# Gate logits of five token tiles as VectorE products instead of TensorE products, in an attention, MLP and mixture-of-experts kernel

## The chip, the cores and the metric

The kernel runs on one core of a Trainium2 chip. The metric is the device time of one launch in microseconds. Five engines work from queues of their own: TensorE (PE in the profile; its weight loads are PEld), VectorE (DVE), ScalarE (ACT), GpSimd (POOL) and SyncE (SP, which here only issues DMAs). Each engine takes its instructions strictly in the order in which the program wrote them.

## The reference

Attention with a window of 128 and 4 sink positions over 1536 tokens (2 batches of 768, 8 heads of 64), then a two-layer MLP, then a top-1 mixture of 8 experts:

```python
x = attention(q, k, v)                     # 1536 x 512
h = x @ w_in                               # 512 -> 2048
x = (np.maximum(h, 0) + alpha * np.minimum(h, 0)) @ w_out
logits = x @ w_gate                        # 1536 x 8
expert_idx = np.argmax(logits, axis=1)
gate_w = softmax(logits)[chosen]
# tokens are put into their expert's rows in order of arrival, up to a capacity
h = np.maximum(einsum('ecd,edf->ecf', disp, w1), 0)
y = einsum('ecf,efd->ecd', h, w2)
out[i] = gate_w[i] * y[expert_idx[i], pos[i]]
```

The step that concerns us is `logits = x @ w_gate`: for each token a dot product of 512 numbers with each of 8 gate columns.

## The kernel before

The program has three stages. Attention comes first (about the first 150 us of the span). The MLP follows, token block by token block: blocks 0 and 1 hold 512 tokens each (four tiles of 128), blocks 2 and 3 hold 256 each. The experts come last. The order of instructions on all engines is written out by hand: where the code emits an instruction is where it stands in its engine's queue, and generators (`next(...)`) weave one part's pieces between another's.

One MLP block is 16 steps (`f` = 0 to 15). In a step TensorE first makes the up product of step f (`mlp_up`, line 350, 12 matmuls into tile `h`), then the down products of step f-2 (`mlp_down`, line 381, tile `acc`). Between them lies `mlp_act`: ScalarE makes `gn` and `g` from `h` (lines 361, 362), VectorE joins them (line 363), ScalarE rounds to `gh` (line 370) and VectorE forms the rest `gl` (line 373). Woven into it is `w_split`: ScalarE and VectorE split a block of weights for a later step into a high part and a low part, both tiles named `r` (lines 259 and 262). In even steps this is the up weight of step f+2, in odd steps a down weight.

The gate belongs to `route`. When the last down product of a block has run (in step 1 of the next block), `route` copies the block's result from PSUM into `x2` (`evacuate`). After that it advances by one piece in each step from step 2 on, always behind that step's `mlp_act` and `mlp_down`. For each tile of 128 tokens one piece holds four transposes of `x2` on TensorE (line 1026, tile `rt`), a copy to SBUF (`xt`), and in the step after it four small matmuls with the gate's weights `wg_sb` (line 1033, tile `lg`, 8 columns; each stands as two records in the trace). Then come softmax, argmax, the place of each token among its expert's rows (tile `pp`, line 1067 on), and an indirect DMA that scatters the rows. So the gate of block 0 runs within block 1's steps, that of block 1 within block 2's.

The attention inputs of block 0, tiles `x0` to `x3` (128 x 1024 each), are read for the last time by the up product of block 0's step 15. Their slots are used again by expert weights (`moe_slot`), from block 3 on.

Of the kernel before, what the change touches and what calls it, by code (L numbers as in the profile page):

```python
# [35 lines left out]
def attention_mlp_moe_kernel(  # L36
# [18 lines left out]
    P = 128  # L55
# [53 lines left out]

    xs = dram.tile([E * RS, XW], F32, name="xs")  # L110

    ctx.enter_context(tc.manual_schedule(engines=MANUAL))


# [26 lines left out]
    TBLK = [(sum(sizes[:n]), w) for n, w in enumerate(sizes)]  # L141
    NBLK = len(TBLK)
    assert sum(sizes) == NT

    def fill_table():

# [343 lines left out]
    def mlp_steps():  # L490

        n_fill = fill_output()
        if not ahead:
            for _ in fill_table():
                pass
        routing, pending, accs = None, [], {}

        def lower(part=None):
            pb, pf, pg = pending[0]
            ts = range(TBLK[pb][1] // P)  # L500
            if pf == 0:
                accs[pb] = [bank("t", f"acc{pb}_{t}", (P, DM)) for t in ts]
            mlp_down(pb, pf, wts[pb, "wo", pf // FG], pg, accs[pb], ts)
            pending.pop(0)
            if pf < KF - 1:
                return None
            routing = route(pb, ts, accs[pb], [])
            next(routing)
            return routing

        first_down = []
        first = first_chunk()

        def down_to(t):

            for pb, pf, pg in pending:
                if pf not in first_down:
                    first_down.append(pf)
                    mlp_down(pb, pf, wts[pb, "wo", pf // FG], pg, accs[pb], [t])

        for bl in range(NBLK):
            last = bl == NBLK - 1
            if last:
                raw_loads()
                splits_to(1)
            for f in range(KF):
                n = bl * len(worder) + f
                conv = convert_at(n)
                next(conv, None)
                for ph in mlp_up(bl, f, wts[bl, "wi", f // FG]):  # L530
                    yield
                if last and f == KF - 1:
                    down_to(0)
                elif len(pending) == LAG:
                    routing = lower() or routing
                pending.append((bl, f, mlp_act(bl, f, ph, split_at(n), conv)))
                if f % 2 and bl == 1:
                    next(n_fill, None)
                if routing is not None and f >= 2:
                    next(routing, None)  # L540
                if last and f >= 2 and f % 2 and f < KF - 1:
                    splits_to(min(split_n[0] + 1, PER))
                    raw_loads()
                if last and f in (KF - 5, KF - 2):
                    next(first)

        prev, TB = [], TBLK[bl][1]
        late = [(pf, pg, t) for pf, pg in [p[1:] for p in pending] for t in range(1, TB // P)]

        def late_down(n):  # L550
            for _ in range(min(n, len(late))):
                pf, pg, t = late.pop(0)
                mlp_down(bl, pf, wts[bl, "wo", pf // FG], pg, accs[bl], [t])

        late_down(TB // P - 1)
        down_to(0)
        r0 = route(bl, [0], accs[bl], prev)
        next(r0)
        late_down(TB // P - 1)
        next(r0)  # L560
        late_down(len(late))
        splits_to(PER)
        raw_loads()

        def first_steps(n):
            for _ in range(n):
                if next(first, got) is got:
                    break

        for t in range(1, TB // P):  # L570
            r1 = route(bl, [t], accs[bl], prev)
            for r, n in zip((r1, r0, r0, r1), FIRST_UP):
                next(r)
                first_steps(n)
            for _ in r0:
                pass
            first_steps(FIRST_UP[4])
            next(r1)
            first_steps(FIRST_UP[5])
            r0 = r1  # L580
        for n in FIRST_UP[6:]:
            next(r0, None)
            first_steps(n)
        for _ in r0:
            pass

        t = slot("r0", F32)
        next_two = ((0, 1), (1, 0))
        for n, ec in enumerate(next_two):
            rows[ec] = t[:, n * DM:(n + 1) * DM]  # L590
            fetch(*ec)
        t = slot("r5", F32)
        rows[0, 0] = t[:, DM:]
        if NCH == 3:
            rows[0, 2] = t[:, :DM]
            fetch(0, 2)
        fetch(0, 0)
        first_steps(99)
        first = first_lower(*got)
        for n, ec in enumerate(next_two):  # L600
            first_steps(FIRST_DOWN[n])
            if n == 0 and NCH > 1:
                turn_in_slot(*ec, "r1", bank("s", "next_x"))
        first_steps(99)
# [3 lines left out]
    with ExitStack() as actx:  # L608
# [246 lines left out]
        for b in range(B):  # L855
            for hp in range(H // 2):
# [3 lines left out]
                for i0 in range(0, NQ, 2):  # L860
# [10 lines left out]
                        units.append(u)  # L871
                    groups.append(t)

        def early_weights():
            split = iter(())
            for n in range(5 if ahead else 0):
                for _ in w_convert_n(n, 2):
                    yield
                    next(split, None)
                for _ in split:  # L880
                    pass
                split = w_split(n, 2) if n < 3 else iter(())
            for _ in split:
                pass
# [29 lines left out]
        for n in range(nu + 11):  # L914
            u = at(units, n)
            norm = iter(())
            if n % 2 == 0 and at(groups, (n - 8) // 2):
                norm = normalise(groups[(n - 8) // 2])
            if at(units, n - 1):
                softmax(units[n - 1], norm)  # L920
            for _ in norm:
                pass
            parts = {"T": p_transposes(units[n - 2]) if at(units, n - 2) else iter(())}
            parts["V"] = values(units[n - 6]) if at(units, n - 6) else iter(())
            for h in range(2):
                parts["QR"[h]] = scores(u, h) if u else iter(())
            for x in WEAVE:
                next(parts[x], None)
            for x in "TQRV":
                for _ in parts[x]:  # L930
                    pass
            if at(units, n - 2):
                p_evacuate(units[n - 2])
            if n % 2 == 0:
                late_transposes(at(groups, (n - 4) // 2), at(groups, (n - 10) // 2))
            elif at(groups, (n - 3) // 2):
                sink_gather(groups[(n - 3) // 2])
            if u:
                st = u.t.st
                sn = st.b * (H // 2) + st.hp  # L940
                s2 = at(sts, sn + 2)
                if u.i == 0 and sn > 0 and at(sts, sn + QA - 1):
                    load_qk(sts[sn + QA - 1])
                if u.i == 1 and st.hp % 2 == 0 and s2:
                    load_v(s2.b, s2.hp // 2)
            if n in FILL_AT:
                next(table, None)
            if ahead and n in (nu - EARLY - 8, nu - EARLY - 2):
                w_load(int(n > nu - EARLY - 8))
            if n == nu - EARLY:  # L950
                nc.vector.tensor_scalar(
                    out=nalpha, in0=alpha_sb, scalar1=-1.0, scalar2=None, op0=ALU.mult
                )
            if n >= nu - EARLY:
                next(early, None)
            if n >= nu and ahead and n_ahead < MLP_AHEAD:
                next(mlp)
                n_ahead += 1
# [36 lines left out]
    def route(bl, ts, acc, prev):  # L995
# [19 lines left out]
            else:  # L1015
                nc.scalar.copy(out, src[:, :DM])

        lg = bank("t" if last else "o", f"lg{nm}")
        lgv = lg[:, :n * E].rearrange("p (t e) -> p t e", t=n)
        for t in range(n):  # L1020
            evacuate(t, x2[:, t, 0:DM], acc[ts[t]])
        yield
        for t in range(n):
            pt = bank("s", f"rt{nm}_{t}")
            for kd in range(KD):
                nc.tensor.transpose(
                    pt[:, kd * P:(kd + 1) * P], x2[:, t, kd * P:(kd + 1) * P], ident
                )
            xt = rpool.tile([P, DM], F32, tag="xt", name=f"xt{nm}_{t}")
            evacuate(t + 1, xt, pt)  # L1030
            yield
            for kd in range(KD):
                nc.tensor.matmul(
                    lgv[:, t, :], xt[:, kd * P:(kd + 1) * P], wg_sb[:, kd, :],
                    start=(kd == 0), stop=(kd == KD - 1), skip_group_check=True,
                )
        yield

        def small3(nm_, dt=F32):
            return rpool.tile([P, 4, E], dt, tag=nm_, name=f"{nm_}{nm}")[:, :n]  # L1040
# [350 lines left out]
```

## Time and profile before

| | |
|---|---|
| median of 3 runs | 611.75 us (610.82 to 613.17) |
| the profiled execution | 610.9 us |
| its span, first to last instruction | 609.2 us |
| PE busy / PEld busy | 586.3 us (96%) / 491.3 us (81%) |
| DVE busy / ACT busy | 398.5 us (65%) / 346.2 us (57%) |
| POOL busy | 83.6 us (14%) |
| granted TensorE clock, mean | 0.996 |

Busy shares are means over stages that have different limits, so the stretch in question is read by itself. In a timeline a row gives the start and the duration of an instruction or of a run of equal ones. Since instructions overlap at their ends, what one costs its engine is read from its start to the start of the next on the same engine, where that engine doesn't idle between them.

### The profile page before, as it was taken

How to read it: one execution, taken by the hardware profiler on the slowest of the kernel's cores; microseconds unless marked ns; L12 is line 12 of the kernel's file. 1: busy time of each engine (PE TensorE's matmuls, PEld its weight loads, DVE VectorE, ACT ScalarE, POOL GpSimd, SP SyncE). 2: the span in 40 equal slices, each digit the busy share in tenths (PEclk: the TensorE clock that was granted, in tenths of full speed). 3: DMA queues.
4: the chain of work that ended last, by engine and by line, in shares of the span. 5: the costliest groups of instructions: out<-in, count | busy, mean ns of one | idle time of the engine just before them, and what ended most of it. 6: DMA issues, size and time to landing. Idle time of an engine off the chain costs nothing. (4 is left out here: it accounts for less than half of the span.)

```text
span 609.2 us, 9106 instructions
## 1 busy us (share of the span) xinstructions
PE 586.3 (96%) x3230; PEld 491.3 (81%) x3230; DVE 398.5 (65%) x794; ACT 346.2 (57%) x642; POOL 83.6 (14%) x128
## 2 busy tenths in 40 slices
PE   7999999999999999999999999999999999999994
PEld 5999998888777888888899898877777777778783
DVE  6578788589999454454565786976326683886240
ACT  5668776475666353434565676855237574675330
POOL 5012423110000000003000110112220211211011
PEclk9999999999999999999999999999999999999998
DMA  7979741215459000001000011424918593994000
GB/s 227 320 219 293 223 126 70 70 69 185 161 172 380 2 0 1 2 0 53 17 1 2 18 67 36 139 88 128 337 69 306 191 358 133 339 356 139 17 22 34
DMA packets 32404, 81.76 MB, mean 134 GB/s; under 512 B 3574, under 2 KB 4134, under 8 KB 32352
## 3 DMA queue, kind: packets, MB, share of 16 engines
q1 hardware_dynamic: 28208, 69.54, 34.8%
q0 software_dynamic: 4144, 11.53, 5.3%
q8 instruction: 31, 0.51, 0.4%
q14 instruction: 21, 0.17, 0.1%
HBM read 66.65 MB, written 16.29 MB: 136 GB/s over the span
## 5 line engine op out<-in xcount | busy, mean ns | idle before, releaser
L350 PE MATMUL h<-x,r 128*128 128x512 f32 (+1 forms) x768 | 149.3, 341 | 3.3 <-DVE r L262 3.1
L350 PEld LDWEIGHTS h<-x,r 128*128 128x128 f32 x768 | 120.2, 189 | 22.3 <-DVE r L262 5.2
L381 PE MATMUL acc<-r,gh 128*128 128x512 f32 x384 | 120.5, 395 | 0.0
L381 PEld LDWEIGHTS acc<-r,gh 128*128 128x128 f32 x384 | 69.9, 188 | 14.3 <-ACT gh L370 0.2
L381 PE MATMUL acc<-r,gl 128*128 128x512 f32 x192 | 75.9, 396 | 0.0
L363 DVE SCALAR_TENSOR_TENSOR g<-gn,nalpha,g 128x512 f32<-128x512 f32 (+1 forms) x64 | 39.3, 615 | 47.5 <-ACT g L362 47.5
L722 PE MATMUL s<-ka,qa 128*128 128x260 f32 x192 | 59.4, 396 | 4.7 <-DMA qa<-in_q_dram 4.4
L361 ACT ACTIVATE gn<-h 128x512 f32<-128x512 f32 (+1 forms) x64 | 31.3, 489 | 53.5 <-PE h L350 53.2
L832 PEld LDWEIGHTS o<-vr,pT 128*128 128x128 f32 x352 | 55.6, 192 | 4.8
L262 DVE TENSOR_TENSOR r<-wo,r 128x1024 fp32r<-128x1024 f32 x31 | 37.9, 1224 | 27.5 <-ACT r L259 27.4
L832 PE MATMUL o<-vr,pT 128*128 128x65 f32 x352 | 53.7, 251 | 0.0
L1218 ACT ACTIVATE hh<-et 128x512 f32<-128x512 f32 x26 | 15.5, 598 | 65.3 <-PE et L1213 58.5
L1104 POOL DMA_INDIRECT xs<-x,slot_i x12 | 14.1, 1178 | 271.1 <-DVE run L1120 151.2
L741 ACT ACTIVATE p<-sx,mn 128x260 f32<-128x260 f32 (+1 forms) x96 | 42.8, 487 | 9.4 <-DVE mn L737 8.9
L259 ACT CAST r<-wo 128x1024 fp32r<-128x1024 f32 (+1 forms) x33 | 33.8, 1023 | 22.7 <-PE acc L381 21.7
L754 PE MATMUL pt<-ident,p 128*128 128x128 f32 x176 | 46.2, 278 | 0.0
L737 DVE CUSTOM_DVE_ANT_0 sx<-s,mask 128x260 f32<-128x260 f32 (+1 forms) x96 | 36.9, 400 | 13.6 <-PE s L722 9.8
L370 ACT CAST gh<-g 128x512 fp32r<-128x512 f32 (+1 forms) x64 | 33.0, 516 | 20.7 <-DVE g L363 20.5
L381 PEld LDWEIGHTS acc<-r,gl 128*128 128x128 f32 x192 | 36.1, 188 | 8.6 <-DVE gl L373 0.2
L262 DVE TENSOR_TENSOR r<-wi,r 128x1024 fp32r<-128x1024 f32 x30 | 36.7, 1222 | 3.6 <-ACT r L259 3.4
L373 DVE TENSOR_TENSOR gl<-g,gh 128x512 fp32r<-128x512 f32 (+1 forms) x64 | 35.3, 552 | 1.6 <-ACT gh L370 1.6
L722 PEld LDWEIGHTS s<-ka,qa 128*128 128x128 f32 x192 | 30.7, 199 | 5.7 <-issue 4.4
(196 smaller groups left out, 1089.5 us busy)
## 6 DMA issues: line engine op xcount, KB each, us to landing
raw_all<-in_w_dram SPq DMA_DIRECT2D x36, 512.0 KB, 6.3
more_raw<-in_w_dram SPq DMA_DIRECT2D x28, 512.0 KB, 6.2
raw_all<-in_w_in_dram SPq DMA_DIRECT2D x8, 1024.0 KB, 5.6
raw_all<-in_w_out_dram SPq DMA_DIRECT2D x8, 1024.0 KB, 5.0
xs<-r SPq DMA_DIRECT2D x8, 771.0 KB, 10.4
rows<-xs POOLq DMA_DIRECT2D x20, 256.0 KB, 5.7
vr<-in_v_dram SPq DMA_DIRECT2D x4, 780.0 KB, 5.1
out_dram<-fill SPq DMA_DIRECT2D x2, 1536.0 KB, 11.5
```

The lines of the kernel that those rows point to most:

```text
L259: nc.scalar.copy(hi[:, x], w[:, x])
L262: eng.tensor_sub(lo[:, x], w[:, x], hi.bitcast(F32)[:, x])
L350: nc.tensor.matmul(ph[:, :TB], wi[wl][:, kk, f0:f0 + P], xT_at(kk, tok, TB, xl), start=(n == 0), stop=(n == 3 * KD - 1),)
L363: nc.vector.scalar_tensor_tensor(out=g, in0=gn, scalar=nalpha[:, f:f + 1], in1=g, op0=ALU.mult, op1=ALU.add)
L370: nc.scalar.copy(gh, g)
L373: nc.vector.tensor_sub(gl, g, gh.bitcast(F32))
L381: nc.tensor.matmul(acc[t], g[a][:, t * P:(t + 1) * P], wo[w][:, f % FG, :], start=(f == 0 and x == 0), stop=(f == KF - 1 and x == 2),)
L722: nc.tensor.matmul(s[:, o:o + w], st.qa[:, h, toks], st.ka[:, c:c + w], start=True, stop=True, skip_group_check=True,)
L737: nc.vector.tensor_tensor_reduce(out=x[:, :w], in0=u.s[h][:, :w], in1=m[:, :w], scale=-scale, scalar=BIG, op0=ALU.add, op1=ALU.min, accum_ ...
L741: nc.scalar.activation(t.p[:, u.ii, h, :w], x[:, :w], AF.Exp, bias=t.mn[:, c:c + 1], scale=-1.0)
L754: nc.tensor.transpose(pt[:, c * P:(c + 1) * P], t.p[:, u.ii, h, u.offs[n]:u.offs[n] + P], ident,)
L832: nc.tensor.matmul(t.o[:, 2 * u.ii + h, :], u.pT[:, w], vr[:, hv * NQ + j, :], start=(not sg and n == 0), stop=(n == len(js) - 1), skip_gr ...
```

## The change

For all four tiles of block 0 and for the first tile of block 1 the transposes, the copy `xt` and the gate matmuls are left out. In their place VectorE runs, for each tile and each expert, one `tensor_tensor_reduce`: `x2` (128 x 512) times the expert's gate row, with the running sum as the logit. That is 32 products for block 0, four per step in steps 2 to 9 of block 1, and 8 for block 1, one per step in steps 2 to 9 of block 2. The other three tiles of block 1 keep the old way, and their logits are copied to join the new ones. Blocks 2 and 3 are as before.

The products need each gate row on all 128 partitions. So in the attention stage (with the scores of unit 23, counted from 0, of 48) TensorE transposes `wg_sb` into 8 rows of 512, ScalarE copies them to SBUF, and SP writes them to a DRAM tile `gate_rows`. At the start of block 1 SP reads them back by four DMAs that repeat two rows over all partitions, into the slots of `x0` to `x3`. `tensor_tensor_reduce` stands in the trace as `CUSTOM_DVE_ANT_0` with a short `DVE_READ_ACCUMULATOR2_ANT` behind it, and in the lists of order as two rows named `ISA`.

```diff
+    gate_rows = dram.tile([E, DM], F32, name="gate_rows")
...
+    gates = []
+    def load_gate():
+        for n in range(E * DM // SW):
+            t = slot(f"x{n}", F32)
+            rows_ = gate_rows.rearrange("(n e) d -> n (e d)", n=E * DM // SW)
+            nc.sync.dma_start(out=t, in_=rows_[n].unsqueeze(0).to_broadcast([P, SW]))
+            gates.extend(t[:, o:o + DM] for o in range(0, SW, DM))
...
         for bl in range(NBLK):
             last = bl == NBLK - 1
+            if bl == 1:
+                load_gate()
...
+        def turn_gate():
+            pt = bank("ax", "gate_t")
+            for kd in range(KD):
+                nc.tensor.transpose(pt[0:E, kd * P:(kd + 1) * P], wg_sb[:, kd, :], ident)
+            gt = ap_s.tile([E, DM], F32, tag="gt", name="gt", bufs=1)
+            nc.scalar.copy(gt, pt[0:E, :DM])
+            nc.sync.dma_start(out=gate_rows, in_=gt)
...
+            if n == FILL_AT[-1] + 3:
+                turn_gate()
...
-        lg = bank("t" if last else "o", f"lg{nm}")
-        lgv = lg[:, :n * E].rearrange("p (t e) -> p t e", t=n)
+        nv, per = {0: (n, 4), 1: (1, 1)}.get(bl, (0, 1))
+        lgv = rpool.tile([P, 4, E], F32, tag="lgv", name=f"lgv{nm}")[:, :n]
+        if nv < n:
+            lg = bank("t" if last else "o", f"lg{nm}")
+            lgp = lg[:, :n * E].rearrange("p (t e) -> p t e", t=n)
+            if nv == 0:
+                lgv = lgp
         for t in range(n):
             evacuate(t, x2[:, t, 0:DM], acc[ts[t]])
         yield
-        for t in range(n):
+        def on_vector():
+            for m in range(nv * E):
+                t, e = divmod(m, E)
+                xg = rpool.tile([P, DM], F32, tag="xt", name=f"xg{nm}_{m}")
+                nc.vector.tensor_tensor_reduce(
+                    out=xg, in0=x2[:, t, 0:DM], in1=gates[e], scale=1.0, scalar=0.0,
+                    op0=ALU.mult, op1=ALU.add, accum_out=lgv[:, t, e:e + 1],
+                )
+                if m % per == per - 1:
+                    yield
+
+        vec = on_vector()
+        for t in range(nv, n):
+            next(vec, None)
             pt = bank("s", f"rt{nm}_{t}")
...
             for kd in range(KD):
                 nc.tensor.matmul(
-                    lgv[:, t, :], xt[:, kd * P:(kd + 1) * P], wg_sb[:, kd, :],
+                    lgp[:, t, :], xt[:, kd * P:(kd + 1) * P], wg_sb[:, kd, :],
                     start=(kd == 0), stop=(kd == KD - 1), skip_group_check=True,
                 )
-        yield
+        for _ in vec:
+            yield
+        if 0 < nv < n:
+            nc.vector.tensor_copy(lgv[:, nv:], lgp[:, nv:])
+        if nv < n:
+            yield
```

The order on TensorE at the end of step 2 of block 1, of the kernel before: `h_3` and `h_4` are the up products of steps 3 and 4, `acc` the down products.

```order
L381 MATMUL acc_3_2518<-r_5_2410,gl_0_2454 128x512
L1026 MATMUL rt_0_0_2544<-ident,x_0_2481 128x128 x4
L350 MATMUL h_3_2551<-x_1_97,r_5_2448 128x512
...
L381 MATMUL acc_3_2518<-r_5_2410,gl_1_2499 128x512
L1033 MATMUL lg_0_2483<-wg_sb,xt_0_0_2549 128x8 x4
L1026 MATMUL rt_0_1_2594<-ident,x_0_2481 128x128 x4
L350 MATMUL h_4_2601<-x_1_97,r_6_2536 128x512
```

The same place of the changed kernel.

```order
L393 MATMUL acc_3_2535<-r_5_2419,gl_0_2471 128x512
L362 MATMUL h_3_2569<-x_1_98,r_5_2465 128x512
...
L393 MATMUL acc_3_2535<-r_5_2419,gl_1_2516 128x512
L362 MATMUL h_4_2616<-x_1_98,r_6_2553 128x512
L362 MATMUL h_4_2616<-x_1_99,r_6_2553 128x512
```

The transposes and the gate matmuls are gone, and the next up product follows the down product directly.

The order on VectorE in steps 2 and 3 of block 1, of the kernel before.

```order
L373 TENSOR_TENSOR gl_2_2542<-g_2_2531,gh_2_2539 128x512
L1014 COPY xt_0_0_2549<-rt_0_0_2544 128x512
L363 SCALAR_TENSOR_TENSOR g_3_2576<-gn_3_2577,nalpha,g_3_2576 128x512
L262 TENSOR_TENSOR r_7_2582<-wo_1_1807,r_6_2581 128x1024
L373 TENSOR_TENSOR gl_3_2587<-g_3_2576,gh_3_2584 128x512
L363 SCALAR_TENSOR_TENSOR g_4_2626<-gn_4_2627,nalpha,g_4_2626 128x512
```

The same place of the changed kernel.

```order
L385 TENSOR_TENSOR gl_2_2559<-g_2_2548,gh_2_2556 128x512
L1058 ISA xg_0_0_2561,lgv_0_2500<-x_0_2498,x_2_2427 128x512
L1058 ISA lgv_0_2500 128x1
L1058 ISA xg_0_1_2563,lgv_0_2500<-x_0_2498,x_2_2427 128x512
...
L1058 ISA xg_0_2_2565,lgv_0_2500<-x_0_2498,x_2_2429 128x512
...
L1058 ISA xg_0_3_2567,lgv_0_2500<-x_0_2498,x_2_2429 128x512
...
L375 SCALAR_TENSOR_TENSOR g_3_2594<-gn_3_2595,nalpha,g_3_2594 128x512
L274 TENSOR_TENSOR r_7_2600<-wo_1_1816,r_6_2599 128x1024
L385 TENSOR_TENSOR gl_3_2605<-g_3_2594,gh_3_2602 128x512
```

Four products stand where at most one copy stood, ahead of the next step's join (line 363 before, 375 in the changed kernel).

The order of SP's DMAs about the start of block 1, of the kernel before.

```order
L201 DMA raw_all<-in_w_out_dram 128x2x1024
L166 DMA out_dram<-fill 128x6x512 x2
L1165 DMA raw_all<-in_w_dram 128x1024 x4
L1165 DMA raw_all<-in_w_dram 128x2x512 x4
L1165 DMA more_raw<-in_w_dram 128x1024 x2
```

The same place of the changed kernel; `x_2` are the new uses of the slots of `x0` to `x3`.

```order
L213 DMA raw_all<-in_w_out_dram 128x2x1024
L154 DMA x_2_2427<-gate_rows 128x1024
L154 DMA x_2_2429<-gate_rows 128x1024
L154 DMA x_2_2431<-gate_rows 128x1024
L154 DMA x_2_2433<-gate_rows 128x1024
L178 DMA out_dram<-fill 128x6x512 x2
L1214 DMA raw_all<-in_w_dram 128x1024 x4
```

The zero fill of the output and the first expert weights now stand behind the four gate loads.

## Rows read from the trace of the kernel before

**Rows 1.** Busy time by engine in three stretches (us, engines, clock, DMA share, GB/s)
```profile
203.00:302.00 99.00, 99.00 (x473) 81.41 (x472) 46.63 (x74) 45.35 (x72) 5.36 (x5) 1.00 0.03 11
302.00:350.00 48.00, 48.00 (x325) 43.36 (x324) 32.09 (x67) 28.31 (x60) 1.68 (x2) 1.00 0.02 7
390.00:609.00 219.00, 205.16 (x1001) 163.58 (x999) 123.32 (x172) 109.71 (x166) 36.86 (x47) 0.99 0.51 180
```

**Rows 2.** Timeline of PE in block 1 (start us, us, engine, line, what)
```profile
214.69 2.97 PE L350 MATMUL h<-x,r 128*128 128x512 f32 x12
...
226.36 0.95 PE L1033 MATMUL lg<-wg_sb,xt 128*128 128x8 f32 x8
227.17 0.63 PE L1026 MATMUL rt<-ident,x 128*128 128x128 f32 x4
227.56 3.02 PE L350 MATMUL h<-x,r 128*128 128x512 f32 x12
...
247.71 3.05 PE L350 MATMUL h<-x,r 128*128 128x512 f32 x12
...
253.41 2.92 PE L350 MATMUL h<-x,r 128*128 128x512 f32 x12
...
258.95 2.93 PE L350 MATMUL h<-x,r 128*128 128x512 f32 x12
```

**Rows 3.** Timeline of PE in block 2
```profile
315.74 1.68 PE L350 MATMUL h<-x,r 128*128 128x256 f32 x12
...
319.85 1.68 PE L350 MATMUL h<-x,r 128*128 128x256 f32 x12
...
330.58 1.59 PE L350 MATMUL h<-x,r 128*128 128x256 f32 x12
...
333.41 1.59 PE L350 MATMUL h<-x,r 128*128 128x256 f32 x12
```

**Rows 4.** Timeline of PE in the attention stage
```profile
85.90 0.38 PE L797 MATMUL pk_x<-ident,xn 128*128 128x128 f32 x2
86.12 0.33 PE L832 MATMUL o<-vr,pT 128*128 128x65 f32 x2
```

**Rows 5.** Timeline of DVE in the attention stage
```profile
86.31 0.42 DVE L737 CUSTOM_DVE_ANT_0 sx<-s,mask 128x260 f32<-128x260 f32 x1
86.66 0.08 DVE L737 DVE_READ_ACCUMULATOR2_ANT mn<- 128x1 f32 x1
...
90.80 0.68 DVE L231 SCALAR_TENSOR_TENSOR wo<-raw_all,wo 128x512 int32<-128x512 int32 x1
91.40 0.42 DVE L737 CUSTOM_DVE_ANT_0 sx<-s,mask 128x260 f32<-128x260 f32 x1
...
96.67 0.28 DVE L737 CUSTOM_DVE_ANT_0 sx<-s,mask 128x128 f32<-128x128 f32 x1
...
96.88 0.28 DVE L737 CUSTOM_DVE_ANT_0 sx<-s,mask 128x128 f32<-128x128 f32 x1
```

**Rows 6.** Timeline of DVE in block 1
```profile
221.56 0.69 DVE L1014 COPY xt<-rt 128x512 f32<-128x512 f32 x1
...
254.69 1.23 DVE L262 TENSOR_TENSOR r<-wo,r 128x1024 fp32r<-128x1024 f32 x1 [1.96 <-ACT r L259]
...
256.44 0.18 DVE L1051 TENSOR_REDUCE mx<-lg 128x4 f32<-128x32 f32 x1
```

**Rows 7.** Timeline of DVE in block 2
```profile
311.57 0.48 DVE L363 SCALAR_TENSOR_TENSOR g<-gn,nalpha,g 128x256 f32<-128x256 f32 x1
...
313.43 0.68 DVE L1014 COPY xt<-rt 128x512 f32<-128x512 f32 x1
```

**Rows 8.** Timeline of PE, last up product of block 0
```profile
198.02 2.97 PE L350 MATMUL h<-x,r 128*128 128x512 f32 x12
```

**Rows 9.** DMA issues: what, queue, count, KB each, median us to landing
```profile
raw_all<-in_w_dram SPq DMA_DIRECT2D x36, 512.0 KB, 6.3
```

**Rows 10.** Waits of SP's queue over the span: us in total, times, longest
```profile
SPq L1165 <- DVE wo L1148: 73.1, 26, 15.0
```

## Prediction

> **What bounds the kernel now.** I read the busy times by stretch first. [...] So TensorE sets the pace, and VectorE has about half of block 1's time free and a third of block 2's. What the timeline shows of TensorE there is the price of the gate in time, not only in busy share: each instruction starts where the one before lets it. What is taken off TensorE comes off the end, as long as VectorE, with the new work, still delivers `gl` and the split weights before TensorE asks for them.
>
> **Removed from TensorE.** In the timeline of block 1 the gate matmuls of a tile run from 226.36 to 227.17, 0.81 us, and the transposes of the next from 227.17 to 227.56, 0.39 us [rows 2]: 1.20 us a tile, 4.8 us for the four tiles of block 0. The check by whole steps: steps 2 to 6 take from 214.69 to 247.71, 33.02 us; a step without gate takes 5.54 (253.41 to 258.95) to 5.70 us (247.71 to 253.41) [rows 2], five of them 27.7 to 28.5, so the gate of block 0 costs 4.5 to 5.3 us. I take 4.9. For the one tile of block 1 a step with gate takes 4.11 us (315.74 to 319.85) and one without 2.83 (330.58 to 333.41) [rows 3]: 1.28 us, against 1.20 by the spacings. I take 1.25. Together 6.15 us, between 5.7 and 6.6. The copies `xt` that go with them (two of ACT's and three of DVE's) were off the path and give nothing.
>
> **Added to TensorE.** Four transposes in the attention stage, 128 columns each. Two such cost 0.22 us from start to next start (85.90 to 86.12) [rows 4], so four cost 0.44. From below it is 0, if they fall into one of the attention's gaps. From above I add one ACT copy of 512 columns, 0.6 us as long as the copy on DVE in rows 6, in case the PSUM bank that they share with the late transposes is not yet free a step later: 1.0 us. I take 0.44, since a whole step lies on either side of them. Behind SP's write of the gate rows stand the next loads of q, k and weights, which wait no more than that copy; they are for work six units on.
>
> **Added to VectorE.** No row before shows a running-sum product of two SBUF tiles of 512 columns. The attention's `CUSTOM_DVE_ANT_0`, the same operation with one operand in PSUM, takes 0.35 us at 260 columns until its accumulator is read (86.31 to 86.66; the reading is 0.08 us long, and the next operation starts beside it) and 0.21 us at 128 until the next product starts (96.67 to 96.88) [rows 5]. That is 1.06 ns a column and 0.07 us fixed, so 0.62 us at 512. An operation on two SBUF operands of 512 columns, without a running sum, takes 0.60 us (90.80 to 91.40) [rows 5]. I take 0.62. The lower bound is 0.60, the upper one double the time per column, as if the two operands were read one after the other: 0.07 + 2 x 0.54 = 1.16 us. The rows show nothing of that kind, so I stay with the value between the two near rows.
>
> In a step of block 1 VectorE has of its own a split and a `gl`, 1.75 us (254.69 to 256.44) [rows 6], and the join, some 0.66 us: 2.41. Four products make 2.48, together 4.9 us of a step of about 5.6. In block 2 the step's own work is 1.86 us (311.57 to 313.43) [rows 7], with one product 2.5 us of at least 2.83. So VectorE keeps up in both, and the price on the path is nothing. But the products stand ahead of the next step's join, and in odd steps the split waits for ScalarE, which waits for the down product; so a join comes up to 1.5 us late. I followed the chain by these durations: in block 1 `gl` is done some 6 us after its up product's end and is wanted two steps later, at 11; the up weight is ready 5 us after and wanted at 8.3. In block 2 `gl` is done at about 4.0 us and wanted at 5.7, the up weight at about 3.3 and wanted at 4.25. The tightest margin is about 1 us, in block 2; if it is gone it costs a few tenths.
>
> What is late next where the gate's stall goes? One thing: in step 3 of block 2 a product now stands ahead of the one copy `xt` that VectorE keeps. It ends then about when TensorE reaches its matmuls. I put it at 0 to 0.1 us.
>
> **The gate loads.** SP waits for the release of `x0` to `x3`, at the end of block 0's last up product: 198.02 + 2.97 = 200.99 [rows 8]. The four DMAs write 512 KB each; loads of that size land 6.3 us after issue in the median [rows 9], and the DMA engines are busy for 3% of that stretch [rows 1]. Estimate: all there by 212. The first product can't start before about 221 (221.56 is the start of the copy whose place it takes [rows 6]). Nine microseconds hide the loads. The repeated read of one pair of rows is in no row of before; only if the four took over 20 us would it show. Behind them in SP's queue stand the zero fill and the first expert weights, wanted from block 3 on, over 100 us later.
>
> **The tail.** The routing of block 0 ends three steps later than before, that of block 1 four. Both still end within their blocks, and the small `pp` products only move. Past 390 us PE is busy for 205 of 219 us with the DMA engines at 51% [rows 1], and the weight loads there are issued when a split has freed their buffer (26 waits of SP on one of the splits' kinds alone [rows 10]). They hang on the engines' progress and not on a fixed moment. So the whole tail moves up with the MLP.
>
> **Sum.** -6.15 + 0.44 = -5.7 us, between -4.7 and -6.6. The profiled execution took 610.9 us, so 605.2 for one like it. The median of before is 611.75, 0.85 above it, and the same difference on the median gives 606.05. I forecast 606.0.
>
> **Rivals.**
> *The products run at half rate.* [...]
> At 1.16 us VectorE would need, from the start of the first product (about 221.2, since TensorE has dropped one set of transposes) to the split that step 12 of block 1 uses, 32 products and 18.7 us of its own work (seven steps of 2.41 and 1.8): 55.8 us. TensorE wants that split after nine steps from 220.3, at 270.9, so 49.7 us later: it stalls for 6.1 us, more than the 5.7 gained, and the result is 612.2, slower than before by a little. The stall begins at (49.7 - 18.7)/32 = 0.97 us a product, and the loss at 1.15. With the accumulator's reading (0.08 us a product [rows 5]) no longer overlapped it would be 1.24 us and 614.7. In block 2 even 1.16 us fits: 3.0 us a step, late by 0.2 a step for four steps.
>
> *Part of the gain is given back.* The late join uses up the margins in block 2, the wait for `xt` grows, or the attention's transposes meet a bank that isn't free. For it: margins of 1 us or less, and SP, ACT and PE all wait somewhere in the attention. Against it: each of these can happen once or a few times, at tenths of a microsecond to 1 us. Together 1.5 to 3.5 us: 607.5 to 609.5.
>
> *The time is lost in the tail.* If the expert stage were paced by its weight loads, the earlier arrival would turn into waits, and the result would be that of before with the transposes on top, 611 to 612. For it: 180 GB/s there, and PE idle for 14 us [rows 1]. Against it: those loads follow the splits [rows 10].
>
> **How the numbers follow.** I give the forecast (604.8 to 607.3) 0.72, the part given back 0.12, the half rate 0.09 and the tail 0.07. A difference of 0.5%, 3.1 us, is about what a measurement of this kernel can tell from no change; it lies at 608.7 and 614.8. Faster by more: the forecast and a half of the second case, 0.78. Slower by more: the worst of the half rate and what I haven't thought of, 0.06. Within: 0.16. For the range I go from 604.3, the largest gain on the profiled execution's own time, to 610.5, which leaves out the half rate and the tail.
>
> **What would show it.** In the profile after, PE should still have no wait in blocks 1 and 2, and steps 3 to 5 of block 1 should take about 5.6 us from up product to up product in place of some 6.85. The products should stand at about 0.62 us from start to start. About 1.1 would speak for the half rate, and then PE would wait for `r` of the split in steps 8 to 12 of block 1. DVE's busy time should grow by about 24 us (40 products of 0.62 to 0.69, less three copies). A first product that waits for a DMA would show the gate loads late. If steps in blocks 1 and 2 are shorter as said but the span isn't, the tail took it: more idle time of PE after 390 us. I am wrong if a product costs over 1 us, or if the whole moves by under 3 us.

## The result, and the profile after

The changed kernel takes 606.54 us in the median (605.23 to 607.41, 5 runs), the kernel before 611.75. The ratio is 0.9911, with a 95% interval from 0.9889 to 0.9933. The profiled execution has a span of 603.4 us against 609.2, so 5.8 us less.

The busy times of the same three stretches as in [rows 1] (the last one ends with the shorter span):

```profile
203.00:302.00 99.00, 99.00 (x453) 80.72 (x452) 67.52 (x141) 46.82 (x74) 3.83 (x4) 1.00 0.21 79
302.00:350.00 48.00, 48.00 (x326) 43.23 (x325) 36.81 (x84) 30.85 (x64) 0.74 (x2) 1.00 0.02 7
...
390.00:603.00 213.00, 199.21 (x964) 158.26 (x962) 118.18 (x164) 104.67 (x155) 34.87 (x45) 0.99 0.52 180
```

PE is as full as before. VectorE went from 46.6 to 67.5 us in block 1 and from 32.1 to 36.8 in block 2. All that was added to it stands beside TensorE's work.

The timeline of PE in block 1: the starts of the up products of steps 0, 2, 3, 4, 7 and 8. They answer to [rows 2], where step 2 starts at 214.69 and step 7 at 247.71.

```profile
204.20 2.91 PE L362 MATMUL h<-x,r 128*128 128x512 f32 x12
...
215.25 2.97 PE L362 MATMUL h<-x,r 128*128 128x512 f32 x12
...
220.87 2.98 PE L362 MATMUL h<-x,r 128*128 128x512 f32 x12
...
226.49 2.88 PE L362 MATMUL h<-x,r 128*128 128x512 f32 x12
...
243.13 2.98 PE L362 MATMUL h<-x,r 128*128 128x512 f32 x12
...
248.75 2.88 PE L362 MATMUL h<-x,r 128*128 128x512 f32 x12
```

Steps 2, 3 and on now take 5.5 to 5.6 us each, as those without a gate did. From step 2 to step 7 it is 27.88 us in place of 33.02: the gate of block 0 was worth 5.14 us. Step 2 itself starts 0.56 us later than before. So much was lost ahead of it.

The timeline of PE in block 2: the up products of steps 0 and 8, and one tile's gate matmuls with what follows them. Step 8 stands in [rows 3] at 330.58.

```profile
295.32 1.59 PE L362 MATMUL h<-x,r 128*128 128x256 f32 x12
...
313.91 1.05 PE L1077 MATMUL lg<-wg_sb,xt 128*128 128x8 f32 x8
314.82 0.63 PE L1070 MATMUL rt<-ident,x 128*128 128x128 f32 x4
...
324.65 1.59 PE L362 MATMUL h<-x,r 128*128 128x256 f32 x12
```

Step 8 starts 5.93 us earlier than before. The gate matmuls in the middle are the one place where the new order is felt: from their start to the next they take 0.91 us (313.91 to 314.82), where those of the kernel before took 0.81 in [rows 2]. Their copy `xt` stands behind a product on VectorE, so the first of them is held up by 0.1 us. The span is shorter by nearly the same 5.8 us, so the tail moved up with the MLP and gave nothing back that counts.

The timeline of VectorE in block 1: two products of step 2, then the split and `gl` of step 3.

```profile
222.12 0.69 DVE L1058 CUSTOM_DVE_ANT_0 xg<-x,x 128x512 f32<-128x512 f32 x1
222.73 0.09 DVE L1058 DVE_READ_ACCUMULATOR2_ANT lgv<- 128x1 f32 x1
222.73 0.69 DVE L1058 CUSTOM_DVE_ANT_0 xg<-x,x 128x512 f32<-128x512 f32 x1
...
227.78 1.23 DVE L274 TENSOR_TENSOR r<-wo,r 128x1024 fp32r<-128x1024 f32 x1 [1.97 <-ACT r L271]
228.92 0.69 DVE L385 TENSOR_TENSOR gl<-g,gh 128x512 fp32r<-128x512 f32 x1
```

A product starts 0.61 us after the one before, with the accumulator's reading beside the next product. The split of step 3 has VectorE idle for 1.97 us until ScalarE has its part; this gap becomes important below.

The waits of PE between 190 and 350 us are one group, and it lies in block 0, where a wait of 0.91 us was before too:

```profile
PE h L362 <- DVE r L274: 0.9, 1, 0.9
```

From 203 to 350 us PE has no wait, neither before nor after.

The four transposes of the gate's weights in the attention stage, with what stands ahead of them and behind them on PE:

```profile
52.19 0.60 PE L736 MATMUL s<-ka,qa 128*128 128x260 f32 x2
52.63 0.60 PE L891 MATMUL gate_t<-ident,wg_sb 128*8 128x128 f32 x4
53.06 0.34 PE L846 MATMUL o<-vr,pT 128*128 128x65 f32 x2
```

The same two neighbours in the kernel before:

```profile
52.07 0.60 PE L722 MATMUL s<-ka,qa 128*128 128x260 f32 x2
52.51 0.33 PE L832 MATMUL o<-vr,pT 128*128 128x65 f32 x2
```

The transposes take 0.43 us. The other 0.12 of the 0.56 us are there already ahead of them (52.19 against 52.07). They are there from the ninth microsecond on (one product of the scores starts at 8.18 us here and at 8.06 before), long before the first new instruction. SP's four gate loads, with their times to landing:

```profile
L154 SPq DMA_DIRECT2D x<-gate_rows x4: 320/381/425, 200.2 to 202.0; - x4
...
DMA to landing us min/median/max: 4.2/5.7/8.2
```

They are issued from 200.2 us on, as the release of `x0` to `x3` allows (SP waits 20.4 us for PE's `h` in all), and the last has landed by about 210. The first product starts at 222.12 and waits for nothing.

### The profile page after: what moved, and what is told of

It is laid out like the page before. It is cut to its first block, busy times and chain, and to the rows that moved or that the text cites. A ratio compares the mean times of both kernels' runs of the same rounds, so it can differ in the third digit from the quotient of the medians.

```text
span 603.4 us, 9071 instructions
## 1 busy us (share of the span) xinstructions
PE 580.9 (96%) x3174; PEld 485.2 (80%) x3174; DVE 419.8 (70%) x872; ACT 346.6 (57%) x641; POOL 83.8 (14%) x128
## 2 busy tenths in 40 slices
DMA packets 32996, 83.86 MB, mean 139 GB/s; under 512 B 3646, under 2 KB 4206, under 8 KB 32944
## 5 line engine op out<-in xcount | busy, mean ns | idle before, releaser
L373 ACT ACTIVATE gn<-h 128x512 f32<-128x512 f32 (+1 forms) x64 | 31.4, 491 | 40.8 <-PE h L362 40.3
```

## The experiments

**Theory A** is that of the prediction: TensorE's queue sets the pace, what is taken off it comes off the end, and VectorE's work is free until a split or a `gl` comes too late for TensorE. The rivals stand in the expectations.

**The added side alone.** The kernel keeps all gate work of TensorE, and the products are made for nothing.

```diff
-        nv, per = {0: (n, 4), 1: (1, 1)}.get(bl, (0, 1))
+        nx, per = {0: (n, 4), 1: (1, 1)}.get(bl, (0, 1))
+        nv = 0
+        lgx = rpool.tile([P, 4, E], F32, tag="lgx", name=f"lgx{nm}")[:, :n]
...
-            for m in range(nv * E):
+            for m in range(nx * E):
...
-                xg = rpool.tile([P, DM], F32, tag="xt", name=f"xg{nm}_{m}")
+                xg = rpool.tile([P, DM], F16, tag="xg", name=f"xg{nm}_{m}", bufs=1)
...
-                    op0=ALU.mult, op1=ALU.add, accum_out=lgv[:, t, e:e + 1],
+                    op0=ALU.mult, op1=ALU.add, accum_out=lgx[:, t, e:e + 1],
```

> The kernel before with only the added side of the change: gate rows prepared and loaded, and the same 40 products on VectorE (their large output in 2-byte numbers for want of room), written to a tile that nobody reads; TensorE keeps all its gate transposes and matmuls. Theory A (TensorE's queue sets the pace, VectorE's products and the gate loads are hidden): before plus the four transposes of 0.44 us, 612.2 us, between 611.7 and 613. Rival B (the products cost something on the path, and the removed part is worth more than the 6.15 us I gave it): 613.5 us or more.

Measured: 612.0 us beside 611.47 of the kernel before, ratio 1.001 (1.0001 to 1.0019), which is 0.6 us (0.1 to 1.2). The added side costs what the four transposes do, within that interval. The up products of steps 2 and 7 in block 1, and of steps 3 and 4 in block 2:

```profile
214.84 2.97 PE L362 MATMUL h<-x,r 128*128 128x512 f32 x12
...
247.86 3.05 PE L362 MATMUL h<-x,r 128*128 128x512 f32 x12
...
311.77 1.67 PE L362 MATMUL h<-x,r 128*128 128x256 f32 x12
...
316.22 1.68 PE L362 MATMUL h<-x,r 128*128 128x256 f32 x12
```

In block 1 steps 2 to 6 take 33.02 us, as before [rows 2]: there the products on VectorE cost TensorE nothing. In block 2 step 3 takes 4.45 us, where a step with gate took 4.11 [rows 3]. Some 0.3 us is lost there; in this step a product stands ahead of the one copy `xt` that VectorE makes. What the change gains is the removal from TensorE.

**Block 0 alone.**

```diff
-        nv, per = {0: (n, 4), 1: (1, 1)}.get(bl, (0, 1))
+        nv, per = {0: (n, 4)}.get(bl, (0, 1))
```

> The changed kernel with the products for block 0 alone; all four tiles of block 1 go by TensorE as before. Theory A: the tile of block 1 was worth 1.25 us, so 606.54 + 1.25 = 607.8 us; its steps 2 to 6 in block 2 take as long as before. Rival (the margins in block 2 are used up and eat that tile's gain): 606.5 us or less.

Measured: 607.64 us, ratio 0.9935 (0.9919 to 0.9950). That is 1.1 us above the changed kernel, in medians that were measured at different times, so the trace has to carry it. Its up products of steps 0 and 8 in block 2:

```profile
295.55 1.59 PE L362 MATMUL h<-x,r 128*128 128x256 f32 x12
...
326.08 1.59 PE L362 MATMUL h<-x,r 128*128 128x256 f32 x12
```

That is 30.53 us, against 29.33 in the changed kernel (295.32 to 324.65): 1.20 us for the tile. Theory A holds, and the margins in block 2 were enough for one product a step.

**How much VectorE can take: six and eight products a step.** In the first every second product of block 0 is run twice, in the second every one (the repeat writes the same logit).

```diff
+                if bl == 0 and m % 2:            # eight a step: if bl == 0:
+                    xg = rpool.tile([P, DM], F32, tag="xt", name=f"xg{nm}_{m}again")
+                    nc.vector.tensor_tensor_reduce(
+                        out=xg, in0=x2[:, t, 0:DM], in1=gates[e], scale=1.0, scalar=0.0,
+                        op0=ALU.mult, op1=ALU.add, accum_out=lgv[:, t, e:e + 1],
+                    )
```

> The changed kernel with every second product of block 0 run twice: 48 instead of 32, six per step. Theory A (what counts is when VectorE delivers the split that step 12 of block 1 uses): from the first product to the start of that step lie 48.9 us in the changed kernel's trace, VectorE's own work in it is 18.6, 48 products of 0.61 make 29.3, together 47.9: no stall, 606.5 us, up to 607.5. Rival C (VectorE's lateness adds up step by step on the path): six products and 2.4 us of own work are 6.06 us a step against 5.6, 0.45 us a step, 3.6 us in eight: 610.1 us.

> The changed kernel with every product of block 0 run twice: 64 instead of 32, eight per step, which is also what one product at half rate would cost (1.22 us). Theory A: 64 x 0.61 + 18.6 = 57.6 us against 48.9: TensorE waits 8.7 us for splits, and the result is 615.2 us, between 613.5 and 616.5, slower than before. Rival D (it is enough that VectorE has free time in the stretch: 31 us idle in block 1, the extra products need 19.5): 606.5 us, no change.

Measured: 607.32 us with six (ratio 0.9936, 0.9919 to 0.9954) and 619.11 with eight (1.012, 1.0104 to 1.0137). With six, the waits of PE between 190 and 360 us:

```profile
PE h L362 <- DVE r L274: 2.3, 3, 1.1
```

0.9 of the 2.3 us is block 0's from before; 1.4 us is new, where Theory A had none. Rival C, with 3.6 us, is out. With eight, PE's timeline at the up products of steps 8, 10 and 12 of block 1 (each is the part of the product behind the wait), and of step 0 of block 2:

```profile
252.55 4.15 PE L362 MATMUL h<-x,r 128*128 128x512 f32 x10 [3.42 <-DVE r L274]
...
268.11 2.61 PE L362 MATMUL h<-x,r 128*128 128x512 f32 x10 [2.67 <-DVE r L274]
...
283.69 4.01 PE L362 MATMUL h<-x,r 128*128 128x512 f32 x10 [4.08 <-DVE r L274]
...
309.08 1.59 PE L362 MATMUL h<-x,r 128*128 128x256 f32 x12
```

Rival D is out: VectorE had 31 us idle in the stretch, the repeats add 23.7 (below), and still TensorE stood for 10.2 us. What counts is which split comes when. Theory A has the mechanism and the place (the splits of even steps, the last of them that of step 12), but its size was too small: no wait with six, 8.7 us of waits and 615.2 us with eight. What it had wrong shows on VectorE's timeline of the run with eight, at the first product, its repeat and the next product, at the split of step 3, and at the split that step 12 uses:

```profile
221.87 0.69 DVE L1058 CUSTOM_DVE_ANT_0 xg<-x,x 128x512 f32<-128x512 f32 x1
...
222.60 0.69 DVE L1064 CUSTOM_DVE_ANT_0 xg_0again<-x,x 128x512 f32<-128x512 f32 x1
...
223.22 0.69 DVE L1058 CUSTOM_DVE_ANT_0 xg<-x,x 128x512 f32<-128x512 f32 x1
...
227.92 1.22 DVE L274 TENSOR_TENSOR r<-wo,r 128x1024 fp32r<-128x1024 f32 x1
...
282.42 1.22 DVE L274 TENSOR_TENSOR r<-wi,r 128x1024 fp32r<-128x1024 f32 x1
```

A repeat, which writes the same logit again, starts 0.73 us after its product; a product with a logit of its own starts 0.61 or 0.62 us after the one before. In the run with the added side, where all products write one large output tile, a product starts 0.73 us after the one before as well, and a copy to another tile 0.61 us after it (313.56 to 314.17). So the repeats are dearer than the products that they stand for. A product and its repeat take 1.35 us and not 1.22, the 32 pairs 43.2, and with VectorE's own 18.6 us that is 61.8 us: just the time from the first product to the end of the last split shown (221.87 to 283.64). VectorE has hardly a gap in it: from 247 to 260 us it is busy for 12.76 of 13 us. In the changed kernel the first matmul of step 12 that needs this split (the third of the up product) starts 49.4 us after the first product. So it comes 12.4 us late. In that are the waits of 10.2 us.

With six, two products and one repeat take 1.96 us, all 48 together 31.4 in place of 29.3, and in step 3 VectorE idles for 1.0 us until ScalarE has its part of the split. That makes 51.0 us; in the trace it is 51.1 (221.77 to 272.89), and the split comes 1.8 us late. If a repeat cost no more than another product it would be about 49.2 us, an estimate from the same numbers, and just in time. So these runs don't show that six products a step with logits of their own would be too many.

Besides, TensorE's granted clock falls after the two longer waits. The busy times of the stretch before and that behind the first wait end with clock, DMA share and GB/s:

```profile
247.00:252.00 5.00, 2.13 (x10) 1.39 (x8) 4.90 (x14) 0.61 (x2) 0.00 (x0) 1.00 0.00 0
252.00:260.00 8.00, 7.45 (x26) 5.99 (x27) 7.86 (x20) 2.75 (x6) 0.00 (x0) 0.79 0.00 0
```

The granted clock is 0.79 in the mean of that stretch, and 0.82 from 285 to 290 us, behind the wait of 4.08 us. The ten matmuls behind the waits of 3.42 and 4.08 us take 4.15 and 4.01 us, where those behind the wait of 2.67 us take 2.61. From there to the next step's start it takes 6.73 us at step 8, where it takes 5.26 at step 10; at step 12 it is 8.55, of which some 1.9 are `pp` (that step takes 7.46 us in the changed kernel, an ordinary one 5.55). So 1.5 and 1.4 us are lost. The first loss lies ahead of step 12 and is part of the 12.4 us, since up to there VectorE sets the time, and at full clock TensorE would have waited that much longer for the next split; the second comes on top. That makes 13.8 us, and by the trace it is 14.0: step 0 of block 2 starts 105.1 us after step 0 of block 1 (203.96 to 309.08), and 91.1 us after it in the changed kernel (204.20 to 295.32). The medians differ by 12.6 us. The profiled execution is the slowest of four (621.28 us, the others 618.55 to 619.21). It lost 1.2 us more in block 3, where the granted clock was 0.50 from 359 to 361 us (0.96 in the mean from 350 to 390 us, and 1.00 there in the changed kernel); there PE had no wait, and its last work before was the small `pp` products and an up product. So this fall of the clock had no wait right before it, and what brings such a fall about these runs don't settle.

**More gain: two tiles of block 1, and the gate rows by DMA.**

```diff
-        nv, per = {0: (n, 4), 1: (1, 1)}.get(bl, (0, 1))
+        nv, per = {0: (n, 4), 1: (2, 2)}.get(bl, (0, 1))
```

> The changed kernel with two tiles of block 1 on VectorE, two products a step, in place of one tile and one product. Theory A (deadlines of the splits): TensorE saves another 1.25 us; VectorE needs 24.9 us from its first product in block 2 to the split that step 12 uses, and idles 1.2 to 2.4 us in odd steps on the way, while TensorE asks for it after about 25.8 us: a wait of 0.3 to 1.5 us. Result 605.3 to 606.8 us, and PE waits for r in block 2, which it doesn't in the changed kernel. Rival D (free time of VectorE in the stretch is enough): no wait, 605.3 us.

Measured: 606.87 us, ratio 0.9926 (0.9913 to 0.9940), no better than the changed kernel. PE's waits in block 2, from its timeline, between step 0 of block 2 and step 0 of block 3:

```profile
296.40 1.59 PE L362 MATMUL h<-x,r 128*128 128x256 f32 x12
...
311.75 1.06 PE L1077 MATMUL lg<-wg_sb,xt 128*128 128x8 f32 x8 [0.71 <-DVE xt L1038]
...
331.51 1.46 PE L362 MATMUL h<-x,r 128*128 128x256 f32 x10 [0.17 <-DVE r L274]
...
337.70 1.45 PE L362 MATMUL h<-x,r 128*128 128x256 f32 x10 [0.26 <-DVE r L274]
...
350.89 1.59 PE L362 MATMUL h<-x,r 128*128 128x256 f32 x12
```

The three waits come to 1.14 us, but they cost more than that: block 2 takes 54.49 us, 0.57 more than the 53.92 of the changed kernel (295.32 to 349.24), though TensorE has a tile less to do. The steps with the waits take 5.06, 3.28 and 3.33 us, and 4.09, 2.82 and 2.82 in the runs where they have none, 1.94 us in all. Rival D is out here as well. The greatest wait is not a split, as I had expected, but a kept tile's `xt`, whose copy stands on VectorE behind the products.

```diff
         def turn_gate():
-            pt = bank("ax", "gate_t")
...
-            nc.sync.dma_start(out=gate_rows, in_=gt)
+            for kd in range(KD):
+                nc.sync.dma_start(
+                    out=gate_rows[:, kd * P:(kd + 1) * P],
+                    in_=w_gate[:, kd, :].rearrange("p e -> e p"),
+                )
```

> The changed kernel with the gate rows turned by four DMAs from the weights in DRAM to the DRAM tile (4096 numbers of 4 bytes), without the four transposes and the ScalarE copy. Theory A: the transposes were worth 0.44 us, so 606.1 us. Rival (the many small pieces hold up the loads of q, k and v queued behind them): PE waits for a DMA in the attention stage, 607 us or more.

Measured: 651.52 us, ratio 1.065 (1.0632 to 1.0668). The rival was right, and by far more than its price. SP's queue, the greatest wait of PE, and the busy times of two stretches:

```profile
44.00 33.85 SPq L890 DMA_DIRECT2D gate_rows<-in_w_gate_dram  x4
```

```profile
PE s L736 <- DMA qa<-in_q_dram: 41.4, 2, 37.5
```

```profile
0.00:60.00 60.00, 56.07 (x395) 50.61 (x396) 42.02 (x167) 39.88 (x104) 13.88 (x47) 1.00 0.86 250
60.00:100.00 40.00, 8.33 (x56) 7.26 (x54) 6.52 (x25) 5.83 (x16) 4.51 (x4) 0.62 0.80 8
```

Four DMAs of 4 KB each, in pieces of 4 bytes (7766 packets under 512 bytes in the whole run, 3646 in the changed kernel), keep SP's queue for 33.85 us. The loads of q and k stand behind them, and TensorE waits 37.5 us for one. From 60 to 100 us the DMA engines are busy for 80% and move 8 GB/s, where they moved 250 before, and the mean granted clock is 0.62. In the sum this cost 45 us, against 0.43 us of transposes.

> Two tiles of block 1 on VectorE and the gate rows turned by DMA. Theory A: the sum of the two, 604.9 to 606.4 us. Rivals as for each.

Measured: 654.04 us, ratio 1.0698 (1.0680 to 1.0717). The loss by DMA covers all else, and the time tells nothing on the two tiles. The trace repeats what the run with two tiles alone showed: block 2 takes 54.50 us (344.58 to 399.08).

The next one moves the routing's piece, by calling it in `mlp_act` between the copy to `gh` and the split's second half.

```diff
         nc.scalar.copy(gh, g)
+        next(between, None)
         next(split, None)
...
-                if routing is not None and f >= 2:
-                    next(routing, None)
```

> As the one with both, and the routing's piece of each step (the products too) is put between the join and the split of that step on VectorE's queue, where VectorE idles in odd steps until ScalarE has its part of the split (2.0 us in block 1, 1.2 in block 2 in the changed kernel's trace), in place of behind gl. Theory A: joins are no longer late, and the wait of 0.3 to 1.5 us in block 2 falls to under 0.5: 604.8 to 605.3 us. Rival: the split of even steps now stands behind the products and comes later by them, so TensorE waits more than with the products behind gl: 605.5 us or more.

Measured: 650.31 us, ratio 1.0643 (1.0626 to 1.0661). It is covered in the same way. In its trace the wait for `xt` is gone, one new wait for a split, of 0.2 us, is left, and block 2 takes 53.00 us (347.09 to 400.09). So I ran the place of the products without the DMA, and the changed kernel beside it on the same chip.

> Two tiles of block 1 on VectorE, gate rows turned by TensorE as in the changed kernel, and the routing's piece of each step put between the join and the split of that step. In the run with two tiles TensorE waited 0.71 us for a copy xt behind two products, and 0.17 and 0.26 us for splits in block 2: 1.14 of the 1.25 us gained. Theory A: the copy now comes before the split and gl, 1.5 us earlier, and that wait goes: the second tile's gain shows, 605.4 us against 606.5 for the changed kernel. Rival: the splits of even steps, now behind the products, come late and eat it again: 606.5 us or more.

> The changed kernel unaltered, beside the one above on the same chip: 606.5 us, as both theories have it; its waits of PE in block 2 none but for the copy xt of at most 0.1 us.

Measured: 604.90 us, ratio 0.9887 (0.9868 to 0.9906), and 604.98 us, ratio 0.9893 (0.9873 to 0.9912). By the times the two can't be told apart. The changed kernel itself took 606.54 us when it was first measured and 604.98 here, where 606.5 was expected, so 1.6 us between medians that were measured at different times mean nothing. By the traces the two can be told apart: steps 0 and 8 of block 2, the one wait of PE there, and step 0 of block 3, with the early products,

```profile
295.04 1.59 PE L362 MATMUL h<-x,r 128*128 128x256 f32 x12
...
322.97 1.59 PE L362 MATMUL h<-x,r 128*128 128x256 f32 x12
...
329.19 1.46 PE L362 MATMUL h<-x,r 128*128 128x256 f32 x10 [0.18 <-DVE r L274]
...
348.05 1.59 PE L362 MATMUL h<-x,r 128*128 128x256 f32 x12
```

and the changed kernel beside it:

```profile
295.23 1.59 PE L362 MATMUL h<-x,r 128*128 128x256 f32 x12
...
324.56 1.59 PE L362 MATMUL h<-x,r 128*128 128x256 f32 x12
...
349.15 1.59 PE L362 MATMUL h<-x,r 128*128 128x256 f32 x12
```

From step 0 to step 8 it is 27.93 us against 29.33: the second tile's gain is there in that stretch. The one wait left, 0.18 us, lies behind it, in step 10, and takes a part back: over the whole of block 2 it is 53.01 us against 53.92, 0.91 us less. The spans of the two profiled executions differ by 1.6 us. That it beats the changed kernel in the median is not shown.

## Why the prediction was right

The forecast was 606.0 us, the result 606.54. Point by point:

- *TensorE sets the pace, and the gate's time there comes off the end.* Shown by the run with the added side alone (no gain without the removal) and by the starts of the steps.
- *The sum.* I had -6.15 and +0.44. By the starts it was -5.14 for block 0 (I took 4.9, between 4.5 and 5.3), and -1.20 for the tile of block 1 (1.25). Another 0.15 us came off between step 7 of block 1 and the start of block 2 (52.34 us before, 52.19 after). The transposes cost 0.43. Two small amounts that I hadn't named went the other way: 0.12 us in the first nine microseconds, and 0.15 between step 0 of block 3 and the end. All together that is the 5.8 us of the spans. That the median came within 0.5 us of the forecast is luck in part, since the same kernel gave 604.98 when it was measured again.
- *The product's price.* 0.62 us from two widths of the same operation with one operand in PSUM, and 0.61 measured with both in SBUF. That a product could run at half rate, 1.16 us, was my estimate for the upper bound, and no run shows it: where products follow each other directly, the most from start to start is 0.73 us, with the same logit or the same large output written again.
- *The cover.* VectorE kept up, and the one wait that I named for a kept tile's `xt`, 0 to 0.1 us, is there with about 0.1. The gate loads had landed some 12 us before their use; I had said nine to spare. VectorE's busy time grew by 21.3 us (398.5 to 419.8), where I had about 24.
- *The tail.* It moved up: from step 0 of block 3 to the end it is 254.2 us, and was 254.0 before. None of the loads of expert weights holds it at a fixed moment.
- *What was mis-sized.* The half-rate rival's working holds where VectorE has no gap. With eight products a step each of the four costs 1.35 us; the working gives 32 x 1.35 + 18.7 - 49.7 = 12.2 us, and the split for step 12 came 12.4 late. With six it is 0.98 us each, which gives 0.4 us, and the split came 1.8 late: in step 3 VectorE idled for 1.0 us, which a count from the first product on leaves out. So near its threshold of 0.97 us a product the working promises too much. Its prices, 612.2 at 1.16 and 614.7 at 1.24, also let TensorE run on at full clock behind the last wait; with eight a step that cost another 1.4 us. No run had a product at just these prices.

## What to carry to other kernels

On an engine that is busy all the time, price work from start to start in the stretch concerned, and move it to an engine with room. Room is not the share of idle time (with eight a step 31 us idle stood against 23.7 us of repeats, and TensorE waited 10.2 us): add up the other engine's work from the first moved piece to each thing that the bound engine asks of it, with the idle gaps that remain, and put the pieces into such a gap if there is one. Take the price of a piece from a row in which it stands as it will stand: a repeat that stood in for a product was 0.12 us dearer than the product, and by the estimate above that decided the run with six. Don't turn a small matrix by a DMA of single numbers on a queue that also feeds the bound engine: here it held the queue for 33.85 us, and the transposes took 0.43.

## What I had not expected of the hardware

- After a wait of 3.4 us in a stretch that had run at full clock, the next ten matmuls took 4.15 us in place of 2.6, and after one of 4.1 us 4.01; after one of 2.7 us they took 2.61. The three short waits of block 2 with two tiles cost more than their length as well: they come to 1.14 us, and the three steps were 1.9 us longer.
- A running-sum product of 512 columns that wrote where the one before wrote (the same logit with eight a step, the same large output in the run with the added side) started 0.73 us after it; with places of its own it started after 0.61 or 0.62, beside the reading of the accumulator.
- Four DMAs of 1024 pieces of 4 bytes each held the issuing queue for 33.85 us, and TensorE waited 37.5 us for a load behind them.
